# Packed attention and routed experts on one core: the stores of the turned attention and of the packed values go from SyncE's queue to GpSimd's

## The chip, the cores and the metric

One NeuronCore of a Trainium2 chip runs the whole kernel. The metric is the device time of one execution in microseconds. The core has five instruction streams that matter here: TensorE (PE in the profile, with its weight loads as PEld), VectorE (DVE), ScalarE (ACT), GpSimd (POOL) and SyncE (SP). Each stream runs its instructions in program order, so an instruction that waits for a semaphore holds back everything behind it on its own engine. A DMA is issued by one of these streams; the issue stands in that stream's order too.

## The reference

The kernel computes a two-step attention and then a mixture of experts with one expert for each token, all in fp32:

```python
p_packed = sm_attn(p, k, v)               # (8, 8, 32, 64): 32 packed rows for each batch and head
out = sm_attn(q, p_packed, p_packed)      # (8, 8, 576, 64)
x = out.transpose(0, 2, 1, 3).reshape(4608, 512)
e = argmax(x @ w_gate)                    # one of 8 experts for each token
y = gate_w * eom[e] * (relu(x @ w1[e]) @ w2[e])
```

Here `gate_w` is the softmax of the gate at the chosen expert, and `eom` is a sigmoid gate of `x @ w_output_gate`.

## The kernel before

**The work of a batch.** There are 8 batches of 576 tokens. A batch goes through three generators and then through the expert's two matrix products.

- `encode(b)` makes the packed values. TensorE forms the scores of `p` against `k`, ScalarE takes the exponentials, VectorE turns them (`a1T`, L314). GpSimd writes a column of ones and zeros into the loaded values `vt` (L308, one copy for each of the two halves g). TensorE then multiplies `a1T` with `vt` into `ps_pp` (the matmul with 80 parts, by the helper at L99). VectorE divides by the sums (`ppc`, L331), and `ppc` is stored to the DRAM tile `pp_d` (L333). TensorE also transposes `ppc` into `ppT` for the further work on the chip.
- `route(b)` makes the attention of the tokens over the 32 packed rows. VectorE turns the scores, subtracts the maximum, sums and multiplies (L409, L426; some of these pieces are on GpSimd), and turns the result into `a2T` (L427), one half g after the other. Each half is stored to the DRAM tile `a2_d` (L429; the profile writes `a_d`) as soon as it is turned: 128 partitions of five runs of 128 fp32, that is 640 runs of 512 B. ScalarE then rounds `a2T` to `ah` (L433), and `al` is the rest (L436, VectorE or GpSimd). TensorE forms the gate's logits from `a2T` (`ps_lg`).
- `weights(b)` loads the expert's weights on SP and splits `w2` into a rounded part `w2h` (ScalarE, L519) and a rest `w2l` (L521, VectorE or GpSimd). `values_up(b)` multiplies the packed values with `w1` (`ps_G`) and splits the result into `Gh` and `Gl`.
- `ffn(b)` is the bulk of TensorE's work: `ps_h` (L92, from `ah`, `al`, `Gh`, `Gl`) and `ps_o` (L618 and L633, from `hT`, `w2h`, `w2l`), and then the stores of the output on SP (L602, L640).

`a2T` is one buffer for all batches, and `ppc` has two. What is stored in `a2_d` and `pp_d` is read again only for tokens whose expert is not their batch's expert: once at about 361 us (`leftover`, L687 and L689, on SP), and in a loop at the end, of which the trace shows no iteration.

**The order of the work is written out by hand.** `ffn(b)` yields after each small step, and the strings START and PLANS say after which step which other generator goes one step on (x and y are `encode` of two batches and of one batch ahead, r and t are `route` of the next and of this batch, w and W `weights`, k, v and q the loads on SP). The order in which instructions are emitted in this way is the order of each engine's stream. `CFG["pool"]` names the pieces that GpSimd does. Beside the stores, GpSimd's stream in this order is, from batch 0's second half of `route` on:

| batch whose store it is | emitted before the store, on GpSimd | the stores | emitted behind it, on GpSimd |
|---|---|---|---|
| 0 | `w2l` of batch 0, j = 2 | `a2T` g = 0, g = 1 | the two `vt` copies of batch 1 |
| 1 | the two `vt` copies of batch 1 | `ppc` | L409 of batch 1 |
| 1 | L426 of batch 1, g = 0 | `a2T` g = 0, g = 1 | `al` of batch 1, g = 0 |
| 2 | `w2l` of batch 1, j = 2 | `ppc` | L409 of batch 2, twice |
| 2 | L409 of batch 2 | `a2T` g = 0 | L426 of batch 2, g = 1 (which `a2T` g = 1 needs) |
| 2 | L426 of batch 2, g = 1 | `a2T` g = 1 | one `vt` copy of batch 3, then `al` of batch 2, twice |
| 3 | `w2l` of batch 2, j = 2 | `ppc` | `w2l` of batch 2, j = 3 |
| 3 | `w2l` of batch 2, j = 3 | `a2T` g = 0 | two `vt` copies of batch 4 |
| 3 | two `vt` copies of batch 4 | `a2T` g = 1 | `al` of batch 3, g = 1 |
| 4 to 7 | `w2l` of the batch before, j = 2 | `ppc` | `w2l` of the batch before, j = 3 |
| 4 to 7 | `w2l` of the batch before, j = 3 | `a2T` g = 0, g = 1 | `al` g = 1, `vt` copies, four `w2l` |

In SP's stream the stores of batch 0's `a2T` stand between the two loads of q for batch 2.

Of the kernel before, what the change touches and what calls it, by code (L numbers as in the profile page):

```python
# [44 lines left out]
def tile_packed_attn_then_moe(ctx, tc, first_in, qT, kp, k2, v, w1, w2, out):  # L45


    nc = tc.nc
# [10 lines left out]
    T = (S + P - 1) // P  # L59
# [15 lines left out]
    def bank(name, tag="a"):  # L75
        return pool.tile([P, BANK], F32, tag=tag, name=name, bufs=NA if tag == "a" else 8 - NA)

    def f(x):
        return x.bitcast(F32)
# [15 lines left out]
    def beside(dsts, seqs):  # L95

        for j, row in enumerate(zip(*seqs)):
            for dst, (a, m) in zip(dsts, row):
                res = nc.tensor.matmul(dst, a, m, start=j == 0, stop=j == len(seqs[0]) - 1)  # L99
        return res  # L100
# [86 lines left out]
    a2_d = tc.dram_tile([B * T, P, NG, P], F32, name="a2_d")  # L187
    pp_d = tc.dram_tile([B, P, P], F32, name="pp_d")
# [3 lines left out]
    def eng(what, *at):  # L192
        return nc.gpsimd if what + ".".join(map(str, at)) in CFG["pool"] else nc.vector
# [38 lines left out]
    def pairs(x, b, hf):  # L232

        t = loaded.pop((x, b, hf)).rearrange("p (c n) -> p c n", c=NPAIR)
        return [t[:, c] for c in range(NPAIR)]

    def scores(b, stat, mov, nm, tag):

        ps = [bank(f"ps_{nm}", tag)[:, :HS] for _ in range(NG)]
        by_head(ps, stat, mov)  # L240
        return ps

    def encode(b):
# [86 lines left out]
        ppc = sb.tile([P, NG, D], F32, tag="ppc", name="ppc", bufs=2)  # L330
        nc.vector.tensor_tensor(ppc, pp[:, :, :D], rs.to_broadcast([P, NG, D]), ALU.mult)  # L331
        ppc = ppc.rearrange("p g d -> p (g d)")
        nc.sync.dma_start(pp_d[b], ppc)  # L333
        yield
        ps = bank("ps_ppT")
        nc.tensor.transpose(ps[:, :P], ppc, ident)  # L336
# [44 lines left out]
    def route(b):  # L381

        ah = sb.tile([P, NG, S], F32R, tag="ah", name="ah", bufs=CFG["at"], **WIDE)
        al = sb.tile([P, NG, S], F32R, tag="al", name="al", bufs=CFG["at"], **WIDE)
        A[b] = (ah, al)

        s2 = [scores(b, packed[b], pairs("q", b, hf), "s2T", "a" if b else "f") for hf in range(2)]
        yield
        rows = [sb.tile([P, 2, HS], F32, tag="row", name="s2", bufs=CFG["row"]) for _ in range(NG)]

        def turn(hf):
            for g in range(NG):
                nc.vector.transpose(rows[g][:, hf], s2[hf][g])

        turn(0)
        yield
        if b:
            turn(1)
            yield
        for part in ([0, 1],) if b else ([0], [1]):  # L400
            ts = slice(part[0] * HS, (part[-1] + 1) * HS)
            n = (ts.stop - ts.start) // NP
            sf = [x.rearrange("p a b -> p (a b)")[:, ts] for x in rows]
            sv = [x.rearrange("p (j n) -> p j n", n=NP) for x in sf]
            sms = []
            for g in range(NG):
                mx = sb.tile([P, S // NP, 1], F32, tag="mx", name="mx", bufs=2)[:, :n]
                nc.vector.tensor_reduce(mx, sv[g], axis=AX.X, op=ALU.max)  # L408
                eng("sub", b, part[0], g).tensor_tensor(sv[g], sv[g], mx.to_broadcast([P, n, NP]), ALU.subtract)  # L409
                yield  # L410
            for g in range(NG):
                nc.scalar.activation(sf[g], sf[g], AF.Exp, scale=QK)  # L412
            yield
            if part == [0]:
                turn(1)
                yield
            both = sb.tile([P, NG, S // NP, 1], F32, tag="sm2", name="sm2", bufs=1)[:, :, :n]
            for g in range(NG):
                sms.append(both[:, g])
                nc.vector.tensor_reduce(sms[g], sv[g], axis=AX.X, op=ALU.add)  # L420
                if g:
                    nc.vector.tensor_scalar_add(both, both, 1e-9)
                    nc.vector.reciprocal(both, both)
                yield
            for g in range(NG):
                eng("mul", b, part[0], g).tensor_tensor(sv[g], sv[g], sms[g].to_broadcast([P, n, NP]), ALU.mult)  # L426
                nc.vector.transpose(a2T[:, g, ts], sf[g])  # L427
                if ts.stop == S:
                    nc.sync.dma_start(a2_d[b * T:(b + 1) * T, :, g].rearrange("t p n -> p t n"),  # L429
                                      a2T[:, g].rearrange("p (t n) -> p t n", n=P))  # L430
                yield
            for g in range(NG):
                nc.scalar.copy(ah[:, g, ts], a2T[:, g, ts])  # L433
            yield
            for g in range(NG):
                eng("al", b, part[0], g).tensor_tensor(al[:, g, ts], a2T[:, g, ts], f(ah[:, g, ts]), ALU.subtract)  # L436
            yield
        lg = bank("ps_lg", "f")[:, :T * NP]
        pgs = R.pop(b).rearrange("p g i e -> p g (i e)")
        toks = a2T.rearrange("p g (t s n) -> p g t s n", s=P // NP, n=NP)  # L440
        beside([lg[s * NP:(s + 1) * NP].rearrange("p (t n) -> p t n", n=NP) for s in range(P // NP)],
               [[(pgs[:, g], toks[:, g, :, s]) for g in range(NG)] for s in range(P // NP)])
        yield
        L = sb.tile([P, T, NP], F32, tag="row", name="L", bufs=CFG["row"])
        nc.vector.transpose(L.rearrange("p t e -> p (t e)"), lg)
        yield from gate(b, L)
# [370 lines left out]
    def place(plan, b):  # L817

        kinds = dict(x=(encode, 2), y=(encode, 1), Y=(encode, 0), r=(route, 1), t=(route, 0), w=(weights, 1), W=(weights, 0),
                     g=(values_up, 1), G=(values_up, 0), l=(first_leftover, 0))  # L820
        for c in plan:
            if c in kinds:
                piece(kinds[c][0], b + kinds[c][1])
            elif c == "d":
                store()
            elif c.isdigit():
                keep_warm(int(c))
            else:
                fetch(c)
# [13 lines left out]
    n = nc.values_load(n_lefti[0:1, 0:1], min_val=0, max_val=B * T * E)  # L843
# [68 lines left out]
```

## Time and profile before

| | us |
|---|---|
| three runs | 395.38, 398.57, 395.37 |
| their median | 395.38 |
| the profiled execution, its own time | 396.21 |
| its span, first to last instruction | 394.6 |
| PE busy in the span | 385.8 (98%) |
| DVE, ACT, POOL busy | 256.7, 185.1, 98.9 |
| mean granted TensorE clock | 0.998 of full speed |

The profiled execution took 1.6 us more than its span and 0.8 us more than the median of the runs. Matmuls are pipelined and overlap in the records, so a busy share of PE near 100% says that the engine did not wait for long, and the distance between starts says how fast it went. Issuing a DMA and waiting for a semaphore are not counted as busy. The profile's sixth part lists the DMA issues by line, with the queue that issued them: SPq, ACTq or POOLq.

### The profile page before, as it was taken

How to read it: one execution, taken by the hardware profiler on the slowest of the kernel's cores; microseconds unless marked ns; L12 is line 12 of the kernel's file. 1: busy time of each engine (PE TensorE's matmuls, PEld its weight loads, DVE VectorE, ACT ScalarE, POOL GpSimd, SP SyncE). 2: the span in 40 equal slices, each digit the busy share in tenths (PEclk: the TensorE clock that was granted, in tenths of full speed). 3: DMA queues.
4: the chain of work that ended last, by engine and by line, in shares of the span. 5: the costliest groups of instructions: out<-in, count | busy, mean ns of one | idle time of the engine just before them, and what ended most of it. 6: DMA issues, size and time to landing. Idle time of an engine off the chain costs nothing.

```text
span 394.6 us, 9676 instructions
## 1 busy us (share of the span) xinstructions
PE 385.8 (98%) x3783; PEld 311.0 (79%) x3783; DVE 256.7 (65%) x716; ACT 185.1 (47%) x424; POOL 98.9 (25%) x86
## 2 busy tenths in 40 slices
PE   8799999999999999999999999999999999999995
PEld 3468886879769796888879897788868897698875
DVE  5678688766868866278563865559664782568412
ACT  2267444844395364634556246642566343632320
POOL 3524013222156011520044012520126010620000
PEclk9999999999999999999999999999999999999999
DMA  7899089909983599234983269522961049101930
GB/s 297 323 396 414 37 274 374 353 11 336 385 256 102 178 322 415 74 137 125 385 331 103 88 214 402 209 79 70 337 221 64 2 151 378 58 29 39 348 145 28
DMA packets 35535, 83.77 MB, mean 212 GB/s; under 512 B 3487, under 2 KB 15137, under 8 KB 35489
## 3 DMA queue, kind: packets, MB, share of 16 engines
q1 hardware_dynamic: 35024, 81.89, 56.8%
q10 hardware_dynamic: 432, 1.26, 0.8%
q8 instruction: 30, 0.49, 0.5%
q14 instruction: 17, 0.13, 0.1%
q0 software_dynamic: 32, 0.00, 0.0%
HBM read 67.93 MB, written 15.27 MB: 211 GB/s over the span
## 4 chain that ended last, share of the span: by engine, by line
PE 94%; DMA 2%; DVE 1%; ACT 0%; SPq 0%; issue 0%; DVEq 0%
PE ps_o L618 46%; PE ps_h L92 25%; PE ps_o L633 8%; PE ps_G L99 4%; PE ps_s L99 3%; PE ps_pp L99 3%; PE ps_s2T L99 2%; PE ps_lg L99 1%; DMA w<-in_w_dram 1%; DMA k<-in_first_dram 1%; PE ps_lo L778 0%; PE ps_lh L762 0%; PE warm L123 0%; PE ps_ppT L336 0%; DVE a1T L317 0%
## 5 line engine op out<-in xcount | busy, mean ns | idle before, releaser
L618 PE MATMUL ps_o<-w2h,hT 128*128 128x512 f32 (+2 forms) x528 | 168.2, 390 | 0.0
L618 PEld LDWEIGHTS ps_o<-w2h,hT 128*128 128x128 f32 x528 | 98.5, 188 | 24.1 <-issue 3.6
L618 PE MATMUL ps_o<-w2l,hT 128*128 128x512 f32 (+2 forms) x264 | 101.8, 386 | 0.0
L580 DVE SCALAR_TENSOR_TENSOR hT<-ps_h,hT 128x256 fp32r<-128x256 f32 x192 | 61.4, 353 | 47.4 <-ACT hT L577 46.9
L521 POOL TENSOR_TENSOR w2l<-wst,w2h 128x1024 fp32r<-128x1024 f32 x27 | 66.7, 2479 | 98.8 <-ACT w2h L519 95.8
L92 PE MATMUL ps_h<-ah,Gh 128*128 128x256 f32 (+1 forms) x256 | 77.8, 304 | 0.2
L92 PE MATMUL ps_h<-ah,Gl 128*128 128x256 f32 (+1 forms) x256 | 75.7, 296 | 0.0
L92 PE MATMUL ps_h<-al,Gh 128*128 128x256 f32 (+1 forms) x256 | 75.7, 296 | 0.0
L577 ACT ACTIVATE hT<-ps_h 128x320 fp32r<-128x320 f32 (+1 forms) x128 | 51.5, 413 | 41.2 <-PE ps_h L92 40.7
L618 PEld LDWEIGHTS ps_o<-w2l,hT 128*128 128x128 f32 x264 | 49.7, 188 | 8.8
L92 PEld LDWEIGHTS ps_h<-ah,Gh 128*128 128x128 f32 x256 | 48.5, 190 | 3.8 <-DVE mx L408 0.8
L92 PEld LDWEIGHTS ps_h<-al,Gh 128*128 128x128 f32 x256 | 48.5, 190 | 0.6
L92 PEld LDWEIGHTS ps_h<-ah,Gl 128*128 128x128 f32 x256 | 48.5, 189 | 0.0
L601 ACT ACTIVATE ob<-ps_o,scm_all 128x512 f32<-128x512 f32 (+1 forms) x28 | 19.2, 686 | 47.2 <-PE ps_o L618 46.5
L519 ACT CAST w2h<-wst 128x1024 fp32r<-128x1024 f32 x32 | 33.5, 1061 | 10.7 <-DMA wst<-in_w_dram 5.0
L436 POOL TENSOR_TENSOR al<-a2T,ah 128x576 fp32r<-128x576 f32 (+1 forms) x10 | 13.1, 1318 | 96.2 <-ACT ah L433 94.1
L84 DVE TENSOR_TENSOR Gl<-ps_G,Gh 128x512 fp32r<-128x512 f32 (+1 forms) x36 | 20.9, 625 | 22.1 <-ACT Gh L83 21.9
L633 PE MATMUL ps_o<-w2h,hT 128*128 128x512 f32 x64 | 25.7, 401 | 0.0
L633 PE MATMUL ps_o<-w2l,hT 128*64 128x512 f32 x64 | 23.8, 392 | 0.0
L412 ACT ACTIVATE s<-s 128x576 f32<-128x576 f32 (+1 forms) x18 | 11.2, 632 | 22.4 <-DVE s L409 19.9
L304 ACT ACTIVATE a<-ps_s,nm 128x144 f32<-128x144 f32 x64 | 18.3, 400 | 4.8 <-DVE nm L273 4.7
L83 ACT CAST Gh<-ps_G 128x512 fp32r<-128x512 f32 (+1 forms) x36 | 17.6, 542 | 3.0 <-PE ps_G L99 2.5
(177 smaller groups left out, 396.3 us busy)
## 6 DMA issues: line engine op xcount, KB each, us to landing
w<-in_w_dram SPq DMA_DIRECT2D x36, 512.0 KB, 5.8
wst<-in_w_dram SPq DMA_DIRECT2D x36, 512.0 KB, 8.7
vt<-in_v_dram SPq DMA_DIRECT2D x14, 650.0 KB, 10.4
q<-in_qT_dram SPq DMA_DIRECT2D x14, 576.0 KB, 4.6
out_dram<-ob SPq DMA_DIRECT2D x31, 256.0 KB, 2.5
a_d<-a2T SPq DMA_DIRECT2D x16, 320.0 KB, 2.9
k<-in_kp_dram SPq DMA_DIRECT2D x7, 640.0 KB, 7.9
k<-in_k_dram SPq DMA_DIRECT2D x7, 576.0 KB, 7.1
```

Source lines behind the costliest of these rows:

```text
L83: (hi_eng or nc.scalar.copy)(hi, src)
L84: (lo_eng or nc.vector).tensor_tensor(lo, src, f(hi), ALU.subtract)
L92: res = nc.tensor.matmul(dst, a, m, start=j == 0, stop=j == len(seq) - 1)
L99: res = nc.tensor.matmul(dst, a, m, start=j == 0, stop=j == len(seqs[0]) - 1)
L304: nc.scalar.activation(a1s[g][:, c * SQ:(c + 1) * SQ], s1[c // 2][g][:, (c % 2) * SQ:(c % 2 + 1) * SQ], AF.Exp, bias=nm[:, g, c:c + 1], sc ...
L519: nc.scalar.copy(hi, st)
L521: eng("w", b, j).tensor_tensor(lo, st, f(hi), ALU.subtract)
L577: nc.scalar.activation(hT[:, :n], ps, AF.Relu)
L580: nc.vector.scalar_tensor_tensor(hT[:, d0:d0 + s1 - s0], ps[:, s0:s1], 0.0, f(hT[:, s0:s1]), op0=ALU.max, op1=ALU.subtract)
L601: nc.scalar.activation(ob[:, cs], ps[:, cs], AF.Copy, scale=sc)
L618: nc.tensor.matmul(ps[:, cs], a, m[:, cs], start=fc == i == 0, stop=fc == FC - 1 and i == 2)
L633: nc.tensor.matmul(ps[:n], a, m, start=i == 0, stop=i == len(seq) - 1)
```

## The change

Two lines change the engine that issues a store. The stores of `ppc` of batches 1 to 7 and all sixteen stores of `a2T` are issued by GpSimd, at the same places of the emitted order; the store of batch 0's `ppc` stays on SP. Nothing else is touched: the plans, `CFG["pool"]`, the buffers and all loads are as before.

```diff
@@ -330,7 +330,7 @@
         ppc = ppc.rearrange("p g d -> p (g d)")
-        nc.sync.dma_start(pp_d[b], ppc)
+        (nc.gpsimd if b else nc.sync).dma_start(pp_d[b], ppc)
@@ -426,7 +426,7 @@
                 if ts.stop == S:
-                    nc.sync.dma_start(a2_d[b * T:(b + 1) * T, :, g].rearrange("t p n -> p t n"),
+                    nc.gpsimd.dma_start(a2_d[b * T:(b + 1) * T, :, g].rearrange("t p n -> p t n"),
                                       a2T[:, g].rearrange("p (t n) -> p t n", n=P))
```

## Rows read from the trace of the kernel before

**Rows 1.** Busy time by stretch: from and to, length, engines, granted clock, DMA share, GB/s.
```profile
27.00:45.00 18.00, 17.92 (x169) 15.19 (x169) 13.35 (x31) 12.34 (x31) 5.64 (x4) 1.00 0.76 308
230.00:257.00 27.00, 27.00 (x304) 21.23 (x304) 15.51 (x49) 16.18 (x36) 9.55 (x7) 1.00 0.79 291
```

**Rows 2.** Chain that ended last, two batches: start, us, what.
```profile
211.29 2.15 PE ps_h L92 x18
...
256.96 2.15 PE ps_h L92 x18
```

**Rows 3.** SP's waits: line, for whom, us in total, times, longest.
```profile
SPq L333 <- DVE ppc L331: 19.8, 6, 9.2
SPq L429 <- DVE a2T L427: 19.5, 7, 7.9
```

**Rows 4.** Timeline of SP, last row: start, us, engine, line, what, how often.
```profile
390.75 0.33 SPq L602 DMA_DIRECT2D out_dram<-ob  x1
```

**Rows 5.** Timeline of GpSimd: the only DMA that GpSimd issues, 128 rows of 512 B.
```profile
384.01 1.20 POOL L787 DMA_INDIRECT out_dram<-l_ob,l_ridi  x1 [36.61 <-DVE l_ob L782]
```

**Rows 6.** The stores' issues on SP, ns min/median/max, and their landing.
```profile
L333 SPq DMA_DIRECT2D pp_d<-ppc x8: 343/344/1011, 13.1 to 298.5; - x8
L429 SPq DMA_DIRECT2D a_d<-a2T x16: 377/394/479, 50.1 to 320.9; - x16
...
DMA to landing us min/median/max: 2.5/2.9/8.7
```

**Rows 7.** Timeline of SP around the stores of batch 0.
```profile
49.76 0.33 SPq L223 DMA_DIRECT2D q<-in_qT_dram  x1
50.14 1.00 SPq L429 DMA_DIRECT2D a_d<-a2T  x2
```

**Rows 8.** Timelines of GpSimd, VectorE and TensorE around batch 0's turned attention.
```profile
35.82 0.36 POOL L308 COPY vt<-real 128x20 f32<-128x20 f32 x2
...
38.84 0.48 DVE L427 STREAM_TRANSPOSE a2T<-s 128x288 f32<-128x288 f32 x1
...
39.70 0.48 DVE L427 STREAM_TRANSPOSE a2T<-s 128x288 f32<-128x288 f32 x1
40.10 1.39 DVE L314 STREAM_TRANSPOSE a1T<-a 128x576 f32<-128x576 f32 x2
...
42.11 1.34 PE L99 MATMUL ps_pp<-vt,a1T 128*32 128x65 f32 x80
```

**Rows 9.** The same timelines around batch 1's.
```profile
63.66 0.77 DVE L427 STREAM_TRANSPOSE a2T<-s 128x576 f32<-128x576 f32 x1
...
65.11 0.78 DVE L427 STREAM_TRANSPOSE a2T<-s 128x576 f32<-128x576 f32 x1
...
65.22 1.44 POOL L436 TENSOR_TENSOR al<-a2T,ah 128x576 fp32r<-128x576 f32 x1 [2.01 <-DMA out_dram<-ob]
...
71.78 0.28 PE L92 MATMUL ps_h<-al,Gh 128*128 128x256 f32 x1
```

**Rows 10.** The same timelines around batch 2's.
```profile
103.97 1.16 POOL L426 TENSOR_TENSOR s<-s,sm 128x576 f32<-128x576 f32 x1 [7.46 <-DVE nm L290]
...
109.96 2.82 POOL L436 TENSOR_TENSOR al<-a2T,ah 128x576 fp32r<-128x576 f32 x2 [4.67 <-ACT ah L433]
...
106.27 0.78 DVE L427 STREAM_TRANSPOSE a2T<-s 128x576 f32<-128x576 f32 x1
...
108.61 0.77 DVE L427 STREAM_TRANSPOSE a2T<-s 128x576 f32<-128x576 f32 x1
...
111.53 0.75 PE L99 MATMUL ps_lg<-a2T,pg 128*32 128x160 f32 x16
...
118.55 0.28 PE L92 MATMUL ps_h<-al,Gh 128*128 128x256 f32 x1
```

**Rows 11.** Timelines in a later batch: the last half turned for batch 5, GpSimd behind it.
```profile
228.78 0.78 DVE L427 STREAM_TRANSPOSE a2T<-s 128x576 f32<-128x576 f32 x1
...
232.19 1.42 POOL L436 TENSOR_TENSOR al<-a2T,ah 128x576 fp32r<-128x576 f32 x1 [19.14 <-ACT ah L433]
```

## The prediction

> **What bounds the kernel now.** I read the busy time by stretch first. From about 27 us on TensorE is busy for all but 0.08 us of the first stretch shown, and for the whole of a stretch in the steady batches, at a granted clock of 1.00 [rows 1]. The chain of waits says the same in another way: the first product of batch 4 starts at 211.29 us and that of batch 5 at 256.96, so a batch costs 45.67 us, and the chain is PE nearly throughout [rows 2]. So two things can change the time. Either TensorE gets an idle time that it does not have now, and then, with no slack behind it, that time is added to the end; or something ahead of 27 us or behind the last product gets shorter. SP does wait at the stores that are moved, 19.5 us for the turned attention and 19.8 us for the packed values [rows 3], but these are waits of a queue whose loads come early enough: no row of TensorE in the steady batches waits for them. The reader should not take those 39 us for a gain.
>
> **What is removed.** SP loses 16 issues of 0.394 us and 7 of 0.344 us [rows 6], 8.7 us over the whole run, and the waits before them. What stood behind them on SP comes earlier; batch 0's stores go at 50.14 us, just behind a load of q that had its buffer free only at 49.76 [rows 7]. Both the loads and the output stores that move up are covered by the dense PE, so I cost this at nothing. The last output store is issued at 390.75 us and nothing of the moved work stands ahead of it there [rows 4]. The bytes are the same. Batch 0's stores, 640 KB, now start about 10 us earlier, in the stretch 27 to 45 us, where the DMA share is 0.76 [rows 1, 7]; the loads in flight there are for later batches, so nothing again.
>
> **What is added.** GpSimd issues 23 stores, and each of its instructions behind one has to wait, first until VectorE has made the data, then while GpSimd makes up the transfer. Call the second time s for a store of turned attention (640 runs of 512 B). The trace has no plain DMA from GpSimd. The nearest row is its indirect one, 1.20 us for 128 rows [rows 5]. If that is all fixed cost, s is 1.2; if it is all per row, s is 5 x 1.20 = 6.0. SP's issue grows only from 344 to 394 ns between the same 128 and 640 runs [rows 6], and in that ratio s would be 1.37. I take 2.0: near the lower end because of SP's ratio and because 1.20 includes reading 128 indices, above it because here instructions of an engine, not SP's queue, write out five times the rows. The ends 1.2 and 6.0 stay for the range. A store of packed values has 128 runs, and I take 1.2 for it.
>
> The Trainium skill ("DMA: Bandwidth & Descriptors", section on the anatomy of one DMA on the GpSimd path) says that descriptor generation is a small part and that many descriptors can be emitted before its incremental cost shows up. By that rule s would stay at the indirect DMA's 1.2 and the sum below would be zero; no run yet shows it.
>
> **Batch 0.** Behind the two stores stand the `vt` copies of batch 1, two in 0.36 us, done at 36.18 us now. The halves of `a2T` are turned at 39.32 and 40.18 [rows 8]. With the change the first store starts at 39.35, the second ends at 39.35 + 2s (for s over 0.85), and the first copy, 0.18 us, ends with 0.05 for the hand-over at 39.6 + 2s. TensorE reads it from 42.11 on, with `ps_pp`, and the second copy only half-way through these 1.34 us. The stall is 2s - 2.5: nothing at s = 1.2, **1.5 us at s = 2**, 9.5 at s = 6. This is the tightest place, because the copies had 6 us of slack and lose 3.5 to waiting for VectorE alone.
>
> **Batch 1.** `al` stands behind both stores. The first half is turned at 64.43, so `al` ends at 64.45 + 2s + 1.44; TensorE reads it at 71.78 [rows 9]. The stall is 2s - 5.9: nothing up to s = 2.9, 6.1 at s = 6.
>
> **Batch 2.** The multiplication of half 1 on GpSimd (L426, 1.16 us) ran at 103.97; now it stands behind the store of half 0, which is turned at 107.05 [rows 10]. Half 1 is then turned at 107.05 + s + 1.16 + 0.77 + 0.1 = 109.1 + s, and TensorE wants it for `ps_lg` at 111.53: a stall of s - 2.4. Behind the second store come a `vt` copy and both `al` (2.82 us), which end at 112.1 + 2s; TensorE reads the first at 118.55 and the second some 0.35 later: 2s - 6.8. The two overlap, so the larger counts: nothing at s = 2, 5.2 at s = 6.
>
> **Later batches.** In batches 4 to 7 the second half is turned as in batch 5, at 229.56, and `al` waits for ScalarE until 232.19 [rows 11]. With s = 2 the second store ends by 231.6, ahead of that; at s = 6 `al` would start near 240 and still be done 15 us before 256.96, where batch 5's product begins [rows 2]. Batch 3 I take with these. A store of packed values ahead of a `w2l` shifts that piece by 1.2 us or less; GpSimd is busy for 9.55 us of the 27 around it [rows 1] and can give that up, so I cost it at nothing. If the cover were gone it would be 1.2 us a batch, in five batches.
>
> **The sum.** 1.5 us, from batch 0 alone. The profiled execution took 396.21 us with a span of 394.6; it would be 397.7 and 396.1. It stands 0.8 above the median of 395.38, so the median comes to 396.9.
>
> **Rivals.**
> - The cost is nearly all fixed, s up to 1.4: no stall at all, 395.4. For it: SP's ratio. Against it: GpSimd's other work grows with its size, from 0.18 us for a copy of 20 elements to 1.16 for a product of 576 [rows 8, 10].
> - **Slower:** s is 3 or more. Then all three early batches stall: at s = 3 the sum is 3.5 + 0.1 + 0.6 = 4.2 us, at s = 4 it is 5.5 + 2.1 + 1.6 = 9.2, at s = 6 it is 9.5 + 6.1 + 5.2 = 20.8, so 399.6, 404.6 and 416.2. It decides from s = 2.9 on. A second store that had to wait for the first one's landing, 2.9 us in the median on SP [rows 6], would do the same. For it: per-row cost and a dense PE. Against it: SP's ratio.
> - VectorE keeps GpSimd from writing out the transfers. Between the two stores of batch 0 VectorE turns `a1T` for 1.39 us and a half of `a2T` for 0.48 [rows 8]; if GpSimd stood still meanwhile, the copies would be 1.9 us later still, so 1.5 + 1.9 = 3.4 and 398.8. The Trainium skill ("SBUF — State Buffer", sections on the two separate sides and on who interferes with whom) says that a DMA from GpSimd's queue is starved while VectorE runs an operation in a two-port mode. The operations that it lists as able to do so are copies, casts and tensor_scalar, not these; no row here shows such a wait.
> - Faster: SP's loads were holding TensorE where the trace does not show it. TensorE's gap-free rows leave only the first 27 us and the 4 us behind 390.75 for that; if the half-microsecond issues of SP there were worth 2 us: 393.4. Against it: the constant 45.67.
> - The change does not do what it says, and the stores leave at the same times: 395.4.
>
> **How the numbers follow.** The forecast (s between 1.4 and 2.9, 395.7 to 398.9) has 0.41, no stall at all 0.22, s over 2.9 has 0.24, VectorE's hold 0.06, faster 0.05, no effect 0.02. The predicted time is the forecast's. A measurement of this kernel can tell about 1%, 4 us, from no change. Slower by more than that takes s over 2.9, with some of VectorE's hold: 0.26. Faster by more than that is the far end of the rival with the loads: 0.03. The rest, 0.71, is the same. The range reaches down to 394.6, past no change by about the scatter of the median, and up to 403.5, s near 3.8; above lie some 0.12, below some 0.05. The forecast's own range is 395.7 to 398.9.
>
> **What would show it.** In the profile of the changed kernel, GpSimd has DMA rows at L429 and L333 whose mean is s. The `vt` copies of batch 1 end near 43.7 us and TensorE idles for some 1.5 us before `ps_pp` of batch 1, with GpSimd's copy as the releaser; from there on its rows stand 1.5 us later and the batches still take 45.67. `al` of batch 1 ends near 70 with no wait behind it, and `ps_lg` of batch 2 does not wait. If the copies end before 42.1, the cost is fixed; if `al` of batch 1 or `ps_lg` of batch 2 releases TensorE late, s is over 2.4. It is wrong altogether if the steady batches change their length, or if stretches before 27 us or behind 390 us do.

## The result and the profile after

The changed kernel takes **397.69 us** in the median of its runs, the kernel before 395.39 beside it: the ratio is 1.0064 (95% interval 1.005 to 1.0077), 2.3 us slower. That is within the 1% called no change in the prediction, but the interval leaves out a ratio of 1. The profiled execution took 398.52 us with a span of 396.9 (before 396.21 and 394.6), so the two traces show the same 2.3 us. From the page of the changed kernel: instructions, busy time by engine, the chain of waits by engine, and the landing of the moved stores.

```profile
span 396.9 us, 9695 instructions
...
PE 387.3 (98%) x3783; PEld 310.7 (78%) x3783; DVE 261.5 (66%) x716; ACT 185.3 (47%) x424; POOL 117.4 (30%) x109
...
PE 89%; DVE 6%; ACT 2%; DMA 1%; issue 0%; DVEq 0%
...
a_d<-a2T POOLq DMA_DIRECT2D x16, 320.0 KB, 4.0
```

GpSimd has 23 more instructions and is busy for 18.5 us more, as it must be. The strange figure is VectorE's: it runs the same 716 instructions and is busy for 4.8 us more (256.7 before), and its share of the chain that sets the end went from 1% to 6%. The groups of GpSimd by line and form give the price of a store (busy us, mean ns of one, idle time before it and what ended that):

```profile
L429 POOL DMA_DIRECT2D a_d<-a2T x16 | 14.3, 896 | 90.7 <-DVE a2T L427 79.1 <-DVE nm L290 8.9 <-DVE estar_i L355 2.7
...
L333 POOL DMA_DIRECT2D pp_d<-ppc x7 | 4.0, 572 | 5.9 <-DVE ppc L331 3.8 <-DMA k<-in_k_dram 2.1
```

So s is 0.90 us for 640 runs and 0.57 for 128. The nearest row before had 1.20 for 128 indirect rows [rows 5]. A store of the turned attention lands 4.0 us after its issue in the median, 2.9 before [rows 6], and no row waits for that. Batch 0 in the changed kernel, GpSimd's and TensorE's timelines:

```profile
39.73 2.02 POOL L429 DMA_DIRECT2D a_d<-a2T  x2 [3.76 <-DVE a2T L427]
41.74 0.64 POOL L308 COPY vt<-real 128x20 f32<-128x20 f32 x2
...
42.20 1.18 PEld L99 LDWEIGHTS ps_pp<-vt,a1T 128*32 128x32 f32 x80 [0.35 <-POOL vt L308]
```

The two stores took 2.02 us together, and the copies did move behind them, as said. GpSimd became the releaser, but `ps_pp` starts at 42.20 where it started at 42.11 [rows 8]: the cover was just enough. The 0.09 us are there before the stores already (the second half of `a2T` is turned at 39.79 instead of 39.70), and TensorE's loader idles 0.35 us ahead of `ps_pp` in both traces, so batch 0 cost nothing.

**Where the 2.3 us are.** Follow one product of TensorE through the batches: `ps_pp` of batch 1 starts 0.09 us later than before, that of batch 2 (79.97 against 79.22 us) 0.75 later, that of batch 3 (122.69 against 120.68) 2.01 later. From there on the offset stays: the last output store is issued at 392.77 us, 2.02 later than at 390.75 [rows 4], and 0.28 us come behind it. So batch 1 lost 0.66 us, batch 2 lost 1.26, and no other batch anything. The chain of the changed kernel (start, us, what), with two of the pieces of VectorE that are new in it, the two whose length has changed, and two products of the steady batches:

```profile
66.70 2.52 DVE al L436
...
113.70 1.87 DVE g_oh L454
...
213.31 2.15 PE ps_h L92 x18
...
258.99 2.15 PE ps_h L92 x18
```

The steady batch is 258.99 - 213.31 = 45.68 us, before 45.67 [rows 2]. The two pieces are a subtraction over 576 elements and a comparison over 40. Before they took 0.78 and 0.20 us; these rows of before were not among those ahead of the prediction (timelines of VectorE, GpSimd and TensorE):

```profile
62.04 1.16 POOL L426 TENSOR_TENSOR s<-s,sm 128x576 f32<-128x576 f32 x1 [4.13 <-DVE g_ne L491]
62.21 1.18 DVE L494 TENSOR_TENSOR g_cnt<-g_cnt,g_ne 128x160 f32<-128x160 f32 x1
...
66.59 0.89 POOL L308 COPY vt<-real 128x20 f32<-128x20 f32 x2
66.62 0.78 DVE L436 TENSOR_TENSOR al<-a2T,ah 128x576 fp32r<-128x576 f32 x1 [0.74 <-ACT ah L433]
...
107.54 0.20 DVE L491 TENSOR_SCALAR g_ne<-iota,estar_all 128x8 f32<-128x8 f32 x1
...
112.97 0.20 DVE L454 TENSOR_TENSOR g_oh<-L,g_mx 128x40 f32<-128x40 f32 x1
...
112.22 1.95 PE L99 MATMUL ps_G<-w,ppT 64*32 64x512 f32 x32
```

Batch 1 in the changed kernel, the same timelines; it answers to [rows 9]:

```profile
66.26 0.88 POOL L429 DMA_DIRECT2D a_d<-a2T  x1 [0.55 <-DVE a2T L427]
67.16 1.44 POOL L436 TENSOR_TENSOR al<-a2T,ah 128x576 fp32r<-128x576 f32 x1
...
66.70 2.52 DVE L436 TENSOR_TENSOR al<-a2T,ah 128x576 fp32r<-128x576 f32 x1 [0.74 <-ACT ah L433]
69.14 2.47 DVE L84 TENSOR_TENSOR Gl<-ps_G,Gh 128x512 fp32r<-128x512 f32 x4
...
71.67 0.72 PE L99 MATMUL ps_s<-k 64*32 64x144 f32 x30 [0.17 <-DVE Gl L84]
```

Both engines do one half of `al`. Before, GpSimd's half ran at 65.22 [rows 9] and was done when VectorE's began at 66.62. Now the stores have pushed GpSimd's half to 67.16, where VectorE's half runs; VectorE's instruction is 2.52 us long and ends at 69.22, 0.62 us behind GpSimd's. `Gl` follows on VectorE at 69.14 instead of 68.37, and TensorE, which had no idle time there, waits for `Gl`.

Batch 2 in the changed kernel; it answers to [rows 10]:

```profile
107.50 0.88 POOL L429 DMA_DIRECT2D a_d<-a2T  x1 [10.23 <-DVE a2T L427]
108.39 1.17 POOL L426 TENSOR_TENSOR s<-s,sm 128x576 f32<-128x576 f32 x1
...
112.72 2.77 POOL L436 TENSOR_TENSOR al<-a2T,ah 128x576 fp32r<-128x576 f32 x2
...
107.70 1.90 DVE L491 TENSOR_SCALAR g_ne<-iota,estar_all 128x8 f32<-128x8 f32 x1
...
110.47 0.77 DVE L427 STREAM_TRANSPOSE a2T<-s 128x576 f32<-128x576 f32 x1
...
113.70 1.85 DVE L454 TENSOR_TENSOR g_oh<-L,g_mx 128x40 f32<-128x40 f32 x1
...
112.95 2.56 PE L99 MATMUL ps_G<-w,ppT 64*32 64x512 f32 x32
...
114.42 0.18 PEld L99 LDWEIGHTS ps_G<-w,ppT 64*32 64x32 f32 x14 [0.41 <-ACT a L304]
...
120.01 0.19 PEld L92 LDWEIGHTS ps_h<-ah,Gh 128*128 128x128 f32 x1 [0.49 <-DVE Gl L84]
```

There are two such meetings. GpSimd's product L426, done at 105.13 before [rows 10], now runs from 108.39 to 109.56, and VectorE's small L491, which stands ahead of the second half's turn, lasts until 109.60. The half is turned at 110.47 instead of 108.61; ScalarE rounds it late, its exponentials (L304) start late, and `ps_G` takes 2.56 us instead of 1.95 because it waits for them. Then GpSimd's two `al` run from 112.72 to 115.49, and the gate's comparison L454 lasts until 115.55; the rest of the gate's chain, `Gh` and `Gl` follow late, and `ps_h` waits.

A held instruction of VectorE shows in the trace as a **long instruction, not as a wait**: look for a group whose mean has grown with the shape unchanged. The kernel before has such holds too. L494 at 62.21 takes 1.18 us where the median of its eight is 0.326, and ends 0.19 us behind GpSimd's product; a piece of L280 at 104.39 takes 0.76 us and ends with GpSimd's product at 105.15. In the changed kernel that product has moved away and the same piece takes 0.16 us. Nothing in the prediction priced these.

The Trainium skill ("SBUF — State Buffer", section on who interferes with whom) says that a VectorE instruction with two inputs in SBUF contends with a GpSimd instruction that reads SBUF, not with one that only writes there, and that the loser is blocked for the whole instruction. The trace agrees for `al` and L454, which read two tiles in SBUF: 1.74 and 1.65 us of extra length, and they end 0.62 and 0.06 us behind GpSimd's piece. L491 reads one tile and a column as its scalar, and it was held by 1.70 us all the same. That need not contradict the Trainium skill: the same section lists `tensor_scalar`, which L491 is, among the operations that can run in a two-port mode and then contend with GpSimd too. No run here shows in which mode L491 ran.

### The profile page after: what moved, and what is told of

It is laid out like the page before. It is cut to its first block, busy times and chain, and to the rows that moved or that the text cites. A ratio compares the mean times of both kernels' runs of the same rounds, so it can differ in the third digit from the quotient of the medians.

```text
span 396.9 us, 9695 instructions
## 1 busy us (share of the span) xinstructions
PE 387.3 (98%) x3783; PEld 310.7 (78%) x3783; DVE 261.5 (66%) x716; ACT 185.3 (47%) x424; POOL 117.4 (30%) x109
## 3 DMA queue, kind: packets, MB, share of 16 engines
q10 hardware_dynamic: 432, 1.26, 0.8%
## 4 chain that ended last, share of the span: by engine, by line
PE 89%; DVE 6%; ACT 2%; DMA 1%; issue 0%; DVEq 0%
PE ps_o L618 42%; PE ps_h L92 25%; PE ps_o L633 8%; PE ps_G L99 3%; PE ps_pp L99 3%; PE ps_s L99 2%; PE ps_s2T L99 2%; PE ps_lg L99 1%; PE warm L123 1%; DMA k<-in_first_dram 1%; DVE Gl L84 1%; ACT Gh L83 1%; DVE al L436 1%; PE ps_lo L778 0%; DVE g_oh L454 0%; PE ps_lh L762 0%
## 5 line engine op out<-in xcount | busy, mean ns | idle before, releaser
L429 POOL DMA_DIRECT2D a_d<-a2T x16 | 14.3, 896 | 90.7 <-DVE a2T L427 79.1
L304 ACT ACTIVATE a<-ps_s,nm 128x144 f32<-128x144 f32 x64 | 18.4, 401 | 4.7 <-DVE nm L273 4.6
```

The lines of the kernel that those rows point to most:

```text
L304: nc.scalar.activation(a1s[g][:, c * SQ:(c + 1) * SQ], s1[c // 2][g][:, (c % 2) * SQ:(c % 2 + 1) * SQ], AF.Exp, bias=nm[:, g, c:c + 1], sc ...
```

## The experiments

In all of them the claim is read at the same three starts of `ps_pp` (batches 1, 2, 3), since what happens before about 42 us shifts by -1.2 to +1.1 us from one profiled execution to the next, and the times of one kernel scatter by more than that. Loss in batch 1 is the distance of the first two starts less that of before (37.11 us), loss in batch 2 that of the last two less 41.46. The last three runs were timed once each, beside 395.55 for the kernel before.

| kernel | starts of `ps_pp`, us | loss in batch 1 | in batch 2 | time, us | ratio to before |
|---|---|---|---|---|---|
| before | 42.11, 79.22, 120.68 | | | 395.39 | |
| changed | 42.20, 79.97, 122.69 | 0.66 | 1.26 | 397.69 | 1.0064 (1.005 to 1.0077) |
| only_a2_b1_b2 | 43.22, 81.02, 123.61 | 0.69 | 1.13 | 397.59 | 1.005 (1.0034 to 1.0065) |
| all_but_a2_b1_b2 | 42.65, 79.75, 121.21 | 0 | 0 | 396.19 | 1.0019 (1.0002 to 1.0035) |
| stores_behind_al | 41.82, 78.95, 120.41 | 0 | 0 | 395.59 | 1.0002 (0.9992 to 1.0012) |
| delay_alone | 41.13, 78.24, 120.48 | 0 | 0.78 | 396.23 | 1.0021 (1.0006 to 1.0036) |
| b1_al_later | 42.17, 79.26, 121.99 | 0 | 1.27 | 397.36 | 1.0034 (1.0017 to 1.0051) |
| b1_al_both_pool | 40.91, 78.02, 120.74 | 0 | 1.26 | 397.28 | 1.005 (1.0035 to 1.0066) |
| gne_two_inputs | 41.20, 78.98, 121.72 | 0.67 | 1.28 | 397.55 | 1.0043 (1.0031 to 1.0054) |
| b2_gap | 41.69, 79.45, 121.70 | 0.65 | 0.79 | 397.52 | |
| b2_mul_first | 41.50, 79.27, 120.73 | 0.66 | 0 | 396.55 | |
| b2_al_vector | 41.18, 78.97, 121.06 | 0.68 | 0.63 | 397.2 | |

### Which stores cost it

Only the `a2T` stores of batches 1 and 2 on GpSimd, and then all the others without these:

```diff
-        (nc.gpsimd if b else nc.sync).dma_start(pp_d[b], ppc)
+        nc.sync.dma_start(pp_d[b], ppc)
...
-                    nc.gpsimd.dma_start(a2_d[b * T:(b + 1) * T, :, g]...
+                    (nc.gpsimd if b in (1, 2) else nc.sync).dma_start(a2_d[b * T:(b + 1) * T, :, g]...
```

> Only the four stores of the turned attention of batches 1 and 2 go through GpSimd; all others are on SyncE as before. Theory 'holding' (the loss arises in batches 1 and 2, where GpSimd's pieces, pushed back by the stores, run beside VectorE instructions and hold them): the whole loss stays, 0.67 us in batch 1 and 1.25 us in batch 2, so 397.3 to 397.8 against 395.4. Theory 'transfers' (the stores on the other queue disturb the loads, in proportion to how many there are): 4 of 23 stores, about 0.4 us, 395.8. Theory 'SyncE' (what moves up in SyncE's stream does it): between the two, since most of SyncE's stores are back.

```diff
-                    nc.gpsimd.dma_start(a2_d[b * T:(b + 1) * T, :, g]...
+                    (nc.sync if b in (1, 2) else nc.gpsimd).dma_start(a2_d[b * T:(b + 1) * T, :, g]...
```

> The complement: 19 of the 23 moved stores stay on GpSimd (all of the packed values, and the turned attention of batches 0 and 3 to 7), those of batches 1 and 2 are back on SyncE. 'Holding': no loss in batches 1 and 2, 395.2 to 395.7, starts of TensorE's rows within 0.2 us of the kernel before. 'Transfers' or 'SyncE': most of the loss stays, 397.

Four of the 23 stores carry the loss: both batches lose with them, neither without them. The second kernel's time, 396.19, is above the 395.2 to 395.7 expected, and its 1.0019 has no counterpart in its batches: its `ps_pp` of batch 1 stands 0.54 us later than before, and the offset stays at 0.53 to 0.54. Whether the stores of batch 0 add something in the head stays open; if they do, it is under the 1.4 us of the interval's upper end.

### The same stores behind GpSimd's pieces

All the stores stay on GpSimd, but those of `a2T` are given out behind `al`:

```diff
-                if ts.stop == S:
-                    nc.gpsimd.dma_start(a2_d[b * T:(b + 1) * T, :, g]...
...
+            if ts.stop == S:
+                for g in range(NG):
+                    nc.gpsimd.dma_start(a2_d[b * T:(b + 1) * T, :, g]...
```

> All stores are on GpSimd as in the changed kernel, but those of the turned attention are emitted behind the two al pieces of their batch, so that GpSimd's product in batch 2 and its al pieces run when they did before. 'Holding': al and VectorE no longer run side by side, 395.2 to 395.7; VectorE's al of batch 1 is back at 0.78 us and its one-hot compare in batch 2 at 0.20. 'Transfers': as the changed kernel, 397.7, since the bytes and the queue are the same. Of late data the same is expected as of holding.

```profile
66.31 1.77 POOL L436 DMA_DIRECT2D a_d<-a2T  x2
...
66.35 0.76 DVE L433 TENSOR_TENSOR al<-a2T,ah 128x576 fp32r<-128x576 f32 x1 [0.74 <-ACT ah L430]
```

The loss is gone from both batches, and the time is that of the kernel before. VectorE's `al` has its normal length right beside two stores: writing out a store does not hold it. This is the best form of the change found, and it gains nothing: with every store of `a2T` off SP, SP's relief is worth 0.

### The delay without any DMA

All stores back on SP. GpSimd instead waits for `a2T` with a copy of one column and fills a small tile five times, in batches 1 and 2; this adds work and leaves none out.

```diff
+    mark = const.tile([P, 1], F32, name="mark")
...
+                    if b in (1, 2):
+                        nc.gpsimd.tensor_copy(mark, a2T[:, g, 0:1])
+                        for _ in range(5):
+                            nc.gpsimd.memset(blank, 0.0)
```

> All stores are on SyncE as in the kernel before; where the stores of the turned attention of batches 1 and 2 stood on GpSimd, a copy of one column of the turned half and five memsets of 128 columns stand instead, about 0.9 us each time, with no DMA. 'Holding': the loss comes back without any transfer, most of 2 us: 396.8 to 397.7, with VectorE's al of batch 1 near 2.5 us. 'Transfers' or 'SyncE': 395.4.

The five fills took 1.25 us, more than a store, so the delay was missized, and the time, 396.23, is below the 396.8 to 397.7 expected. In batch 1 GpSimd's `al` came so late (66.59) that VectorE's was done before it, and there was no loss. In batch 2 the meeting took place, without a store of the change near it:

```profile
65.37 1.26 POOL L435 MEMSET blank<- 128x128 f32 x5
...
65.62 0.76 DVE L441 TENSOR_TENSOR al<-a2T,ah 128x576 fp32r<-128x576 f32 x1 [0.74 <-ACT ah L438]
...
108.18 0.78 DVE L428 STREAM_TRANSPOSE a2T<-s 128x576 f32<-128x576 f32 x1 [1.05 <-POOL s L427]
...
111.25 1.98 PE L99 MATMUL ps_G<-w,ppT 64*32 64x512 f32 x32
...
110.51 2.79 POOL L441 TENSOR_TENSOR al<-a2T,ah 128x576 fp32r<-128x576 f32 x2
...
112.00 1.35 DVE L459 TENSOR_TENSOR g_oh<-L,g_mx 128x40 f32<-128x40 f32 x1
```

So a delay of GpSimd's readers is enough for a loss (0.78 us); the DMA is not needed. VectorE waited 1.05 us for GpSimd's late product here, L496 (the L491 of the changed kernel) was not held, and `ps_G` kept its length but for 0.03 us: the loss lies behind `ps_G`, where the comparison was held.

### Batch 1: later still, and with VectorE's half gone

Late data and a held VectorE both follow from a pushed-back `al`. Six fills behind batch 1's stores make GpSimd's `al` later still:

```diff
+                if b == 1 and g == 0:
+                    for _ in range(6):
+                        nc.gpsimd.memset(blank, 0.0)
```

> The changed kernel, with six memsets of 128 columns (about 1 us) on GpSimd between the stores of batch 1 and GpSimd's al of batch 1, which so starts near 68.1 us instead of 67.2. 'Holding': VectorE's own al of batch 1, which starts at 66.7, is through before GpSimd's starts, is back at 0.78 us, and the 0.67 us of batch 1 are gone although GpSimd is later still: about 397.0. 'Late data' (TensorE waits for what GpSimd makes): the loss of batch 1 grows by the 1 us: about 398.7.

```profile
66.24 0.88 POOL L429 DMA_DIRECT2D a_d<-a2T  x1 [0.56 <-DVE a2T L427]
67.11 1.53 POOL L438 MEMSET blank<- 128x128 f32 x6
68.62 1.43 POOL L439 TENSOR_TENSOR al<-a2T,ah 128x576 fp32r<-128x576 f32 x1
...
66.69 0.76 DVE L439 TENSOR_TENSOR al<-a2T,ah 128x576 fp32r<-128x576 f32 x1 [0.74 <-ACT ah L433]
```

A delay of 1.46 us more removes the loss of batch 1. For batch 1 that rules out late data: it is where the pieces meet that counts, not when GpSimd's ends. The other way to part them is to give both halves to GpSimd:

```diff
-                 "sub2.0.1", "al0.0.0", "w2.3", "mul1.0.0", "sub0.0.1", "sub0.0.0", "al2.0.1", "sub2.0.0",
+                 "sub2.0.1", "al0.0.0", "w2.3", "mul1.0.0", "sub0.0.1", "sub0.0.0", "al2.0.1", "al1.0.1", "sub2.0.0",
```

> The changed kernel, with VectorE's al of batch 1 given to GpSimd as well, so that GpSimd has two of 1.44 us behind the stores, the second ending near 70.0 us. 'Holding': VectorE starts Gl about 68.4 as in the kernel before, the 0.67 us of batch 1 are gone: about 397.0. 'Late data': the second al ends 1.4 us later than the one now, and the loss of batch 1 grows: 398 to 399.

```profile
67.17 2.48 DVE L84 TENSOR_TENSOR Gl<-ps_G,Gh 128x512 fp32r<-128x512 f32 x4 [2.49 <-ACT Gh L83]
```

GpSimd's two halves take 2.83 us from 65.88 on, and `Gl` starts on VectorE at 67.17 with its usual 2.48 us. Batch 1 loses nothing, batch 2 its 1.26 as before. `Gl` reads `ps_G` and `Gh`, one of them not in SBUF (`ps_G` is an output of TensorE, in PSUM), and is not held by GpSimd's reading. Both times, 397.36 and 397.28, are above the 397.0 expected. By its ratio the first kernel is 1.3 us slower than the kernel before, as its starts say; the second is 2.0 us slower (1.4 to 2.6), and what its time has beyond the 1.26 us of its starts is not explained.

### Does the form of the small instruction matter?

L491 is a tensor_scalar. Written as a tensor_tensor of the same size:

```diff
-        nc.vector.tensor_scalar(ne[:, 0], iota[:, 0], estar_all[:, b:b + 1], None, ALU.not_equal)
+        nc.vector.tensor_tensor(ne[:, 0], iota[:, 0], estar_all[:, b:b + 1].to_broadcast([P, E]), ALU.not_equal)
```

> The changed kernel, with the compare of the expert number (L491, a tensor_scalar of 128x8) written as a two-input compare. In the changed kernel it took 1.90 us at 107.70, while GpSimd's store ran from 107.50 to 108.38 and its product from 108.39 to 109.56. If the store itself holds a tensor_scalar but not a two-input operation, the compare now takes 0.2 us at 107.7 and a later one of the same chain is held by the product instead; the second half of batch 2 is turned 0.4 to 0.6 us earlier and TensorE gains 0.3 to 0.6 us: 397.2. If only the product holds VectorE, the chain ends as late as before: 397.7.

```profile
107.41 1.17 POOL L426 TENSOR_TENSOR s<-s,sm 128x576 f32<-128x576 f32 x1
...
106.72 1.90 DVE L491 TENSOR_TENSOR g_ne<-iota,estar_all 128x8 f32<-128x8 f32 x1
```

It is held for the same 1.90 us and nothing is gained. The hoped-for repair failed: here the form with a scalar operand and the form with a second tile were held alike.

### Batch 2: the two holds apart

Two fills between the first store and the product L426. The fills went over 128x128 elements, not over 128x576 as the expectation says, 0.49 us together:

```diff
+                    if b == 2 and g == 0:
+                        for _ in range(2):
+                            nc.gpsimd.memset(blank, 0.0)
```

> The changed kernel, with two fills of a 128x576 tile on GpSimd between batch 2's first store of the turned attention and GpSimd's product L426 of the second half; a fill writes and reads nothing. In the changed kernel VectorE's small compare L491 stood at 107.70 for 1.90 us, beside the store (107.50, 0.88) and the product (108.39, 1.17). If it is the reading piece directly behind the store that holds VectorE, the compare is back at about 0.2 us beside the store and the fills; GpSimd's product comes at least 1 us later, so the second half is turned as late as now or later, and batch 2 loses 1.2 to 2.5 us in place of 1.26. If the store itself holds VectorE, the compare takes 0.9 us or more. Batch 1 loses 0.67 us as before by both.

```profile
106.97 0.87 POOL L429 DMA_DIRECT2D a_d<-a2T  x1 [10.24 <-DVE a2T L427]
107.84 0.49 POOL L433 MEMSET blank<- 128x128 f32 x2
108.29 1.15 POOL L426 TENSOR_TENSOR s<-s,sm 128x576 f32<-128x576 f32 x1
...
107.18 0.20 DVE L494 TENSOR_SCALAR g_ne<-iota,estar_all 128x8 f32<-128x8 f32 x1
...
109.48 0.78 DVE L427 STREAM_TRANSPOSE a2T<-s 128x576 f32<-128x576 f32 x1 [1.16 <-POOL s L426]
...
112.45 2.48 PE L99 MATMUL ps_G<-w,ppT 64*32 64x512 f32 x32
```

L491 (L494 here) is back at 0.20 us beside the same store: it is the reading piece directly behind a store that holds VectorE, not the store. The loss came to 0.79, under the 1.2 to 2.5 expected, since the fills were smaller than that sum took them: the half was turned 0.5 us earlier than in the changed kernel (109.48 against 110.47, less the 0.52 by which the two runs' `ps_pp` of batch 2 differ), and the comparison L454 was held to 1.38 us instead of 1.85.

`ps_G` still took 2.48 us although L491 was not held: here VectorE waited 1.16 us for the product itself. So in batch 2 a late product alone can cost TensorE as well. In the changed kernel the product ended at 109.56 and the half was turned from 110.47 on, so without the hold the turn would come some 0.9 us earlier (an estimate from these two rows). Measured against `ps_lg` that is 0.25 us later than before the change, and in the kernel with the delay alone the turn was 0.53 us later by this measure with `ps_G` at 1.98 (in the run here it was 0.63 us later). That puts the longer `ps_G` of the changed kernel down to the hold, by argument and not by a run of its own.

Now the first store of batch 2 behind the product, all else as in the change:

```diff
+                if b == 2 and g:
+                    nc.gpsimd.dma_start(a2_d[b * T:(b + 1) * T, :, 0]...
...
-                if ts.stop == S:
+                if ts.stop == S and (b, g) != (2, 0):
```

> The changed kernel, with batch 2's first store of the turned attention given out behind GpSimd's product L426 of the second half; nothing else is moved. By the theory that GpSimd's readers, pushed back by stores, hold VectorE: the product is at its old place, the compare L491 takes 0.2 us, the second half is turned about 1.1 us earlier than in the changed kernel, and TensorE's ps_G does not wait (0.6 us of the loss gone). Both al of batch 2 still stand behind the stores, which now follow each other, so VectorE's L454 may still be held: batch 2 loses 0.1 to 0.7 us in place of 1.26. If the stores cost TensorE by what they move or by a queue, batch 2 loses 1.26 as before. Batch 1 loses 0.67 by both.

```profile
107.22 0.20 DVE L494 TENSOR_SCALAR g_ne<-iota,estar_all 128x8 f32<-128x8 f32 x1
...
113.02 0.36 DVE L457 TENSOR_TENSOR g_oh<-L,g_mx 128x40 f32<-128x40 f32 x1
```

L491 (L494 here) is back at 0.20 us beside the store. Moving one store behind one product removes all of batch 2's 1.26 us, more than expected: with the half turned on time, `al` on GpSimd ends early enough that L454 is held by 0.16 us only, and that is covered. Last, both `al` of batch 2 on VectorE:

```diff
-                 "sub2.0.1", "al0.0.0", "w2.3", "mul1.0.0", "sub0.0.1", "sub0.0.0", "al2.0.1", "sub2.0.0",
-                 "w0.2", "mul2.0.1", "al2.0.0", "mul0.0.0"))
+                 "sub2.0.1", "al0.0.0", "w2.3", "mul1.0.0", "sub0.0.1", "sub0.0.0", "sub2.0.0",
+                 "w0.2", "mul2.0.1", "mul0.0.0"))
```

> The changed kernel, with both al of batch 2 done by VectorE in place of GpSimd; the stores stand as in the changed kernel. By the theory that GpSimd's readers hold VectorE: the product L426 still stands behind the store and holds L491 for 1.9 us, so ps_G is still late by about 0.6 us; the second hold (L454, 1.85 us beside GpSimd's al) is gone and L454 takes 0.2, but VectorE itself has two more pieces of 0.78 us in front of or behind the gate's chain. Batch 2 loses about 0.6 us in place of 1.26, up to 1.4 if the al come ahead of the chain. If the second part of the loss has another cause than GpSimd's al, it stays at 1.26 with L454 at 0.2. Batch 1 loses 0.67 by both.

```profile
106.71 1.90 DVE L491 TENSOR_SCALAR g_ne<-iota,estar_all 128x8 f32<-128x8 f32 x1
...
112.73 0.20 DVE L454 TENSOR_TENSOR g_oh<-L,g_mx 128x40 f32<-128x40 f32 x1
...
111.97 2.53 PE L99 MATMUL ps_G<-w,ppT 64*32 64x512 f32 x32
```

The second hold is gone, the first stands with `ps_G` at 2.53 us, and the loss is 0.63: half of 1.26. The first hold, with the late product behind which it stands, costs the 0.6 us in `ps_G` and sets up the second, which costs the rest.

## Why the prediction was right and where it was wrong

The time came out 0.8 us above the forecast of 396.9, inside its own range of 395.7 to 398.9, and the sign was right. The reason given for it was not.

- **What bounds the kernel: right.** A dense TensorE passes on every idle time: the 2.01 us by which batch 3's `ps_pp` is late stand unchanged at 392.77 us.
- **SP's relief costed at nothing: right.** Of the 39 us of waits at the moved stores [rows 3] 2.7 are left on SP, at the one store that stayed, and the kernel with all stores of `a2T` behind `al` takes as long as before.
- **The term s: too large.** Taken as 2.0 between 1.2 and 6.0, it measured 0.87 to 1.13, mean 0.90, below the lower end; the packed values took 0.57 for 1.2. The indirect row [rows 5] was no lower bound. SP's ratio, 1.15, was closer to the real 0.896 / 0.572 = 1.57 than five times. The rule of the Trainium skill ("DMA: Bandwidth & Descriptors", anatomy of one DMA on the GpSimd path), that many descriptors come before their cost shows, agrees with the trace only in part: five times the runs made a store 57% longer, 0.32 us.
- **Batch 0, the whole sum of 1.5 us: wrong.** With s = 0.90, 2s - 2.5 is negative, and even with the 2.02 us that this pair took `ps_pp` came only 0.09 us later. The copies, which were to end near 43.7, ended at 42.38. This is the failed step: the entire forecast hung on it, and its range (s between 1.4 and 2.9) did not contain the s that was measured. The range's upper end was added up too low as well: at s = 2.9 its own formulas give 3.3 us for batch 0 and 0.5 for batch 2, so 399.2 and not 398.9.
- **Batches 1 and 2, costed at nothing: wrong, 0.66 and 1.26 us.** The formulas 2s - 5.9, s - 2.4 and 2s - 6.8 asked when GpSimd's results would be late for the first product of TensorE that reads them, and they were right in that: `ps_lg` of batch 2 started at 112.27, only the 0.74 us late that it carried from batch 1. They did not ask what VectorE does at the new places of GpSimd's readers, nor who else waits for the half that VectorE turns: ScalarE rounds it ahead of the exponentials for which `ps_G` waits, and `ps_G` was 0.6 us longer with `ps_lg` on time.
- **Later batches nothing: right**, 45.68 us for 45.67. **Bytes and landing nothing: right.**
- **The rivals.** "The cost is nearly all fixed, s up to 1.4" had its bound on s right and its conclusion, 395.4, wrong. "Slower, s of 3 or more" is out. "VectorE keeps GpSimd from writing" had the two engines right and the direction reversed: fifteen of the sixteen stores of `a2T` took 0.87 to 0.91 us, and only the first of batch 0 took 1.13, so the stores were not held by more than some 0.25 us, against the 1.9 of that rival. It was VectorE that stood still.

That the time and its sign came out near the forecast is luck: a stall of 1.5 us that did not come was replaced by two of together 1.9 that were not foreseen.

## What to carry to other kernels

When a step moves onto GpSimd's queue, price not only when GpSimd's later pieces become ready but what VectorE runs at their new places: a GpSimd piece that reads SBUF and is pushed back by a store of 0.9 us can lengthen a 0.2 us instruction of VectorE to 1.9. Give such a store out behind GpSimd's reading pieces, not ahead of them; here that one move took the whole loss back. Look for VectorE groups whose mean grows at an unchanged shape (L491, L454) before looking at waits, and distrust a forecast whose sum hangs on one unmeasured price.

## What the runs showed of the hardware

- VectorE was held **before the reading piece is recorded as started**. In the changed kernel L491 started at 107.70 and would have ended at 107.90, but GpSimd's product is recorded only from 108.39, behind a store that ran until 108.38; in batch 1 VectorE's `al` began at 66.70, 0.46 us ahead of GpSimd's, and still lost. With fills between store and product the hold was not there. The Trainium skill ("GPSIMD Engine Reference", section 2.1, instruction dispatch) says that GpSimd's cores do not wait for each other between instructions, each starting the next one when its own share is done; cores that have no part in a store could so already be in the product. No run here shows the cores, so this stays a reading. By the rule of "SBUF — State Buffer" in the Trainium skill (who interferes with whom) whoever issues first has the ports; by the recorded starts that would have been VectorE both times, so either those starts are not the ones that count or the rule fails here, and the measured 2.52 and 1.90 us decide what to expect.
- Fills by GpSimd do not hold VectorE's two-input instructions: `al` took 0.76 us beside them in the delay kernel.
- The hold goes the other way too. In the kernel before, GpSimd's two `vt` copies at 66.59 took 0.89 us beside VectorE's `al` (66.62, 0.78 us); two of them took 0.36 at 35.82 [rows 8].
- Whether a short copy behind a store (the `vt` copy, 0.23 us) holds VectorE early is open: in the kernel with the stores behind `al`, L454 (L455 there) took 0.20 us beside the stores, but it was done at 112.91, 0.94 us before the copy began, while L491 had started 0.69 us ahead of the product that held it.
